# A block of sliding-window attention and a gated MLP on one core: the last bank's causal masks go to VectorE, the input sums start later, and one more gate/up tile leaves the attention stage

## The chip, the cores and the metric

The kernel runs on one core of one Trainium2 chip. The metric is device time in microseconds (us) of the whole program. Three runs of the kernel before took 1064.9, 1059.14 and 1061.83 us, a median of 1061.83 us.

Names used below: PE is TensorE, ACT is ScalarE, DVE is VectorE, POOL is GpSimd, and SP is the engine whose queue issues nearly all transfers. Each engine carries out its own list of instructions strictly in order.

## The reference

For an input x of 2048 tokens by 640 channels the kernel computes a normalised input xn and the sum of three things:

```
xn  = layernorm(x)
q, k, v = split(xn @ wqkv)                  # 32 heads of 20 channels
p   = softmax(q k^T / sqrt(20)), key j visible to query i where 0 <= i - j < 256
out = x + (p v) @ wo
        + (gelu(xn @ w_gate) * (xn @ w_up)) @ w_down      # 1728 hidden channels
```

Everything is float32 to the accuracy of three products per multiplication: each operand is split in a high part and a low part, and high*high, low*high and high*low are summed.

## The kernel before

The program has a start (layer norm, transposes, first projections), an attention stage, a gate/up stage and a last stage of output products.

**Attention stage.** The 32 heads form 8 groups of 4, the tokens 4 chunks of 512 queries. A pair of group and chunk is a *unit*, u = 4 * group + chunk, and there are 32 units (`NU`). The loop `attention()` cuts a unit into 14 *slots* (`NS`). All engines but SP have an order written out by this loop, slot after slot. In a unit stand:

- Score maxima. `max_pair` multiplies queries and keys into two PSUM tiles `ps_m` (L480) and lets DVE reduce each one under the mask tile (L490). There are four `ps_m` buffers. A unit has 8 such pairs: two pairs at slots 5 and 9, and four at slot 0, two of them ahead of the product with v and two behind it.
- Exponentials. `exp_piece` writes scores to `ps_e` (L545) and ACT writes their exponentials to a tile `P` (L547). Twelve pieces, two at each odd slot from 1 to 11, fill three *banks* of four heads each. `pieces(c)` says which key blocks lie in which bank. In the kernel before, the banks are called X, Z, Y in that order, so Y comes last.
- Masks. `clear` runs one slot after a bank is full (slots 4, 8 and 12) and zeroes the entries outside the window with POOL instructions (L558 on the diagonal, L561 at the window's tail), each on 128 rows and 4 x 128 columns. Banks X and Y need three masks each and Z two; in chunk 0 it is two, three and one.
- Product with v. `av_unit` of unit u stands at slot 0 of unit u+1: PE multiplies P by v into `ps_o` (L586), 96 instructions in the trace (64 in chunk 0). `steps_` orders the key blocks.
- Filler. `pull_fill` adds `RATE` / 14 matmuls of other work per slot: the remaining projections of q, k and v and gate/up tiles (`gate_up_fill`), written with L105 into `ps_d` or `ps_v`. The list `sets` orders it. `NFA` says how many of the 14 gate/up tiles have all their columns computed here, in 30 matmuls of 512 columns per chunk, three products for each of 5 row blocks for gate and up.
- Transfers. `load_stack(u+3)` reads the stacked q and k of a later unit back from memory, k at slot 9 (`KSLOT`) and q at slot 12, six transfers each. `x_sums` lets POOL make 8 groups of 10 sums of the input's columns (L724), which the next stage uses; group i starts at slot `XS0 + XSN * i`, one sum every second slot.

**Gate/up stage.** After the last unit the remaining gate/up tiles are computed by `gate_up_pair`, two chunks at a time, with seven half products instead of eight: 54 matmuls of 512 columns for two chunks (L935, `ps_g`) where the filler uses 60. It needs the sums that `x_sums` stored. The last, narrower tile is computed between (`gate_up`, 60 matmuls).

**Last stage.** The outputs are multiplied by w_down and wo (L1202), again with seven products where it can.

The tile scheduler fixes only SP's order here; it places SP's transfers in the order in which it expects them to be ready.

Of the kernel before, what the change touches and what calls it, by code (L numbers as in the profile page):

```python
# [9 lines left out]
F32 = mybir.dt.float32  # L10
# [3 lines left out]
OP = mybir.AluOpType  # L14
# [5 lines left out]
C = 512  # L20
# [7 lines left out]
NEG = -3.0e38  # L28
SR = 3 * DH
QROWS = 64 + SR  # L30
NS = 14
RATE = 35.3
V1_SLOT = 169
MXD = 7
KSLOT = 9
LAG = 3, 5, 4, 4, 4, 4, 3, 3, 4, 3, 2, 1, 1, 1
NFA = 4
HD = D // 2
# [3 lines left out]
WARM = 64  # L42
XS0, XSN = 24, 50
RAMP = 4.0
# [21 lines left out]
def block_kernel(ctx, tc, x, wqk, wv, wgu, wdo, wdl, out):  # L66
    nc = tc.nc
# [57 lines left out]
    mask = st1.tile([128, 320], F32, name="mask")  # L125
    low = qkp.tile([128, C], F32, name="r", tag="r", bufs=1)[:, 0:320]
    for m, off in ((mask, 0), (low, 64)):
        nc.gpsimd.memset(m, 0.0)
        nc.gpsimd.affine_select(out=m, in_=m, pattern=[[1, 320]], compare_op=OP.is_ge,
                                fill=NEG, base=off - 1, channel_multiplier=-1)  # L130
        nc.gpsimd.affine_select(out=m, in_=m, pattern=[[-1, 320]], compare_op=OP.is_ge,
                                fill=NEG, base=256 - off, channel_multiplier=1)
# [379 lines left out]
    def pieces(c):  # L512
        b = 4 * c
        X = [(b, 0, 0, 384)] + ([(b - 2, 384, 0, 128)] if c else [])
        Y = [(b + 1, 0, 128, 384), (b + 3, 384, 384, 128)]
        Z = ([(b - 1, 0, 0, 256)] if c else []) + [(b + 2, 256, 256, 256)]
        return X, Z, Y

# [32 lines left out]
    def clear(u, bi):  # L551
        c = u % NC
        pt = pts[u, bi]
        for p in pieces(c)[bi]:
            for col, diag in diag_tail(*p, c):
                a = pt[:, :, col:col + 128]
# [7 lines left out]
    def av_unit(u):  # L564
# [5 lines left out]
        def half(d, r):  # L570
            i = 2 * d + r
            return d, r, max(0, 64 * i), min(C, 64 * i + 320)

        steps_ = [((0, 0), (0, 1)), ((2, 0), (-1, 1)), ((-1, 0), (2, 1)), ((1, 0), (1, 1)),
                  ((3, 0), (-2, 1)), ((-2, 0), (3, 1))]
        todo = [half(*x) for pair in steps_ for x in pair if x[0] in place]
# [189 lines left out]
    NU = NG * NC  # L766
# [22 lines left out]
    def attention():  # L789
# [16 lines left out]
        for u in range(NU + 1):  # L806
            for i in range(NS):
# [678 lines left out]
```

## Time and profile before

| what | value |
|---|---|
| median of three runs | 1061.83 us |
| the profiled execution | 1063.24 us, span 1061.5 us |
| PE busy | 1040.6 us (98% of the span) |
| DVE busy | 737.3 us (69%) |
| ACT busy | 529.4 us (50%) |
| POOL busy | 372.5 us (35%) |
| mean granted clock of PE | 0.997 |
| first product with v starts | 107.88 us |
| gate/up stage starts (L105 into ps_g) | 583.65 us |
| last stage starts | 817.83 us |

In a group of instructions, the numbers behind the bar are the group's busy time, the mean time of one instruction in ns, and the idle time of the engine just before it with what ended most of that. In a timeline, the columns are start, duration, engine, line and what is written from what; brackets hold idle time before it. In a chain of waits they are start, duration and what ran. PE's matmuls overlap one another, so their mean duration is longer than the step from one to the next.

### The profile page before, as it was taken

The page shows a single profiled execution, that of the slowest core. Times are in us where ns is not written, and L with a number is a line of the kernel's source. Part 1 is how long each engine was busy: PE and PEld are TensorE (multiplying, and loading weights), DVE is VectorE, ACT ScalarE, POOL GpSimd, SP SyncE. Part 2 cuts the span into 40 slices and gives each one's busy share as a digit, 9 for nine tenths or more (in the row PEclk, how much of TensorE's full clock was granted, in tenths as well). Part 3 has the DMA queues.
Part 4 walks back from the last instruction along what each step waited for, and adds up shares of the span by engine and source line. Part 5 has one row for each costly group of instructions (what it writes and reads, how often), then busy time and mean ns, then how long its engine had stood idle before and what let it go on. Part 6 is the DMA issues. An engine that isn't in the chain of part 4 may idle for free.

```text
span 1061.5 us, 25594 instructions
## 1 busy us (share of the span) xinstructions
PE 1040.6 (98%) x9405; PEld 834.0 (79%) x9405; DVE 737.3 (69%) x2007; ACT 529.4 (50%) x1120; POOL 372.5 (35%) x534
## 2 busy tenths in 40 slices
PE   8999999999999999999999999999999999999998
PEld 8878656666678765666666888888888999999998
DVE  7845656665655666687674578877655879988887
ACT  4434667666566665666657532322334543433332
POOL 6021777877564658484846021110110000000000
PEclk9999999999999999999999999999999999999999
DMA  5643355564443335443422647576317874343433
GB/s 197 189 129 94 104 156 146 168 183 128 145 125 100 94 104 170 135 139 97 139 82 67 191 164 250 201 258 230 122 50 259 261 243 134 125 136 101 133 123 111
DMA packets 105191, 158.75 MB, mean 150 GB/s; under 512 B 15420, under 2 KB 60092, under 8 KB 105064
## 3 DMA queue, kind: packets, MB, share of 16 engines
q1 hardware_dynamic: 102680, 150.95, 44.4%
q10 hardware_dynamic: 2384, 6.16, 1.8%
q8 instruction: 74, 1.21, 0.5%
q14 instruction: 53, 0.43, 0.1%
HBM read 101.78 MB, written 54.92 MB: 148 GB/s over the span
## 4 chain that ended last, share of the span: by engine, by line
PE 77%; POOL 6%; DVE 6%; DMA 3%; ACT 3%; SPq 2%; issue 2%; ACTq 0%; DVEq 0%; POOLq 0%
PE ps_g L935 21%; PE ps L1202 17%; PE ps_d L105 17%; PE ps_v L105 6%; PE ps_e L545 6%; PE ps_o L586 4%; PE ps_m L480 4%; POOL pt L247 2%; POOL tx L724 1%; PE ps_g L105 1%; DVE junk L490 1%; POOL P L561 1%; ACT P L547 1%; POOL P L558 1%; POOL wql L627 1%
## 5 line engine op out<-in xcount | busy, mean ns | idle before, releaser
L490 DVE CUSTOM_DVE_ANT_0 junk<-ps_m,mask 128x320 bf16<-128x320 f32 (+2 forms) x512 | 243.1, 475 | 150.8 <-PE ps_m L480 94.4
L547 ACT ACTIVATE P<-ps_e 128x512 f32<-128x512 f32 (+2 forms) x384 | 198.8, 571 | 67.7 <-PE ps_e L545 66.1
L1202 PE MATMUL ps<-wb,at 128*128 128x320 f32 x999 | 156.9, 309 | 1.0 <-DVE at L1040 0.8
L1202 PEld LDWEIGHTS ps<-wb,at 128*128 128x128 f32 x999 | 148.9, 188 | 2.2 <-DVE at L1040 1.3
L545 PE MATMUL ps_e<-qs,ks 124*128 124x128 bf16 (+2 forms) x704 | 117.9, 278 | 1.2 <-ACT P L547 0.9
L558 POOL TENSOR_SCALAR_AFFINE_SELECT P<-P 128x512 f32<-128x512 f32 x128 | 83.4, 652 | 86.8 <-ACT P L547 82.7
L105 PE MATMUL ps_d<-xh,wqh 128*128 128x512 f32 x350 | 109.3, 420 | 0.0
L105 PE MATMUL ps_d<-xh,wql 128*128 128x512 f32 x350 | 108.7, 420 | 0.0
L105 PE MATMUL ps_d<-xl,wqh 128*128 128x512 f32 x350 | 108.4, 418 | 0.0
L1202 PE MATMUL ps<-wt,at 128*128 128x320 f32 x552 | 89.2, 310 | 0.8 <-DVE xr L1225 0.8
L545 PEld LDWEIGHTS <-ks 124*128 124x128 bf16 x704 | 49.7, 98 | 50.4 <-issue 37.3
L586 PE MATMUL ps_o<-P,v 64*32 64x320 f32 (+4 forms) x2816 | 77.6, 349 | 7.7 <-POOL P L561 7.4
L1202 PEld LDWEIGHTS ps<-wt,at 128*128 128x128 f32 x552 | 82.9, 188 | 1.4 <-DVE xr L1225 1.0
L1156 ACT ACTIVATE at<-ss 128x512 fp32r<-128x512 f32 x59 | 37.3, 632 | 86.6 <-DVE ss L1040 86.6
L561 POOL TENSOR_SCALAR_AFFINE_SELECT P<-P 128x512 f32<-128x512 f32 x112 | 72.3, 656 | 21.8 <-ACT P L547 21.8
L98 POOL TENSOR_TENSOR wql<-wr,wqh 128x640 fp32r<-128x640 f32 x11 | 17.6, 1606 | 174.1 <-PE ps_g L935 149.5
L586 PEld LDWEIGHTS ps_o<-P,v 64*32 64x32 f32 x2816 | 46.6, 106 | 36.8 <-POOL P L561 12.4
L105 PEld LDWEIGHTS ps_d<-xh,wql 128*128 128x128 f32 x350 | 64.4, 191 | 12.1 <-issue 1.4
L105 PEld LDWEIGHTS ps_d<-xl,wqh 128*128 128x128 f32 x350 | 63.8, 190 | 11.8 <-issue 1.5
L105 PEld LDWEIGHTS ps_d<-xh,wqh 128*128 128x128 f32 x350 | 63.7, 190 | 11.7 <-issue 1.9
L247 POOL TENSOR_TENSOR pt<-r,pt 128x512 bf16<-128x512 f32 x40 | 46.6, 1165 | 73.5 <-ACT pt L246 65.0
L592 ACT ACTIVATE ob<-ps_o 128x512 f32<-128x512 f32 x32 | 19.1, 598 | 92.7 <-PE ps_o L586 75.8
(195 smaller groups left out, 1923.3 us busy)
## 6 DMA issues: line engine op xcount, KB each, us to landing
hr<-hd SPq DMA_DIRECT2D x104, 128.0 KB
hd<-he SPq DMA_DIRECT2D x50, 256.0 KB
wr<-wgu SPq DMA_DIRECT2D x27, 320.0 KB
qs<-qd SPq DMA_DIRECT2D x64, 120.0 KB
ks<-kd SPq DMA_DIRECT2D x64, 120.0 KB
xi<-x SPq DMA_DIRECT2D x16, 320.0 KB
qs<-qd SPq DMA_DIRECT2D x64, 80.0 KB
ks<-kd SPq DMA_DIRECT2D x64, 80.0 KB
```

The costliest lines, as they stand in the source:

```text
L105: nc.tensor.matmul(ps, a(k), b(k), start=n == 0, stop=n == 3 * nk - 1)
L247: nc.gpsimd.tensor_tensor(out=pt[:, l, :], in0=r, in1=pt[:, 1, :], op=OP.subtract)
L480: nc.tensor.matmul(ps[64 * h:64 * h + 64, col:col + w], q[rows, j, q0:q0 + 64], ks_, start=True, stop=True, tile_position=(64 * r, 64 * h))
L490: nc.vector.tensor_tensor_reduce(out=junk[:, 0:n], in0=ps[:, 320 - n:320], in1=mask[:, 320 - n:320], scale=1.0, scalar=NEG, op0=OP.add, op ...
L545: nc.tensor.matmul(ps[:, col:col + n], k[0:QROWS, j, kc:kc + 128], q[0:QROWS, j, q0:q0 + n], start=True, stop=True)
L547: nc.scalar.activation(pt[:, j, lo:hi], ps[:, lo:hi], AF.Exp, scale=SCALE)
L558: nc.gpsimd.affine_select(out=a, in_=a, pattern=[[0, 4], [1, 128]], compare_op=OP.is_ge, fill=0.0, base=0, channel_multiplier=-1)
L561: nc.gpsimd.affine_select(out=a, in_=a, pattern=[[0, 4], [-1, 128]], compare_op=OP.is_ge, fill=0.0, base=-1, channel_multiplier=1)
L586: nc.tensor.matmul(os[r][32 * j:32 * j + 32, qa:qb], v[rows, w0_:w0_ + 32], pt[rows, j, col + qa - q0:col + qb - q0], start=r not in begun ...
L935: nc.tensor.matmul(ps, i, j, start=first and n == 0, stop=n == len(work) - 1, skip_group_check=True)
L1156: nc.scalar.activation(hi[:, 3:7], s, AF.Copy)
L1202: nc.tensor.matmul(ps[bank][:, 0:HD], *work[bank][j], start=bank not in begun, stop=final[p, bank] == n and j == len(work[bank]) - 1, skip ...
```

## The change

Four things change together.

1. The order of the banks becomes X, Y, Z. Z, with two masks (one in chunk 0), is now the last. `clear` treats it differently: DVE, not POOL, clears it, in two instructions for each mask, one for rows 0 to 63 and one for rows 64 to 127, each 4 x 64 columns wide. Only the 64 columns that lie on the edge for those rows are touched, since the product with v reads no others there. The instruction adds a large number to the mask tile and takes the minimum with P. The mask tile grows by four columns for it. `steps_` reads the key blocks of X and Y first and those of Z last. The four instructions stand on DVE at slot 12.
2. k is loaded at slot 12 together with q (`KSLOT` 12), because bank Z, the last reader of the old k, is now the last bank.
3. The sums of the input start at slot 170 with a step of 33 slots in place of slot 24 and 50.
4. `NFA` goes from 4 to 3: gate/up tile 3 leaves the filler and becomes a tenth tile of `gate_up_pair`. That takes 120 matmuls out of the attention stage and adds 108 to the next one. `RATE` falls from 35.3 to 31.2, so each unit gets 4.1 fillers less.

```diff
-RATE = 35.3
+RATE = 31.2
-KSLOT = 9
+KSLOT = 12
-NFA = 4
+NFA = 3
-XS0, XSN = 24, 50
+XS0, XSN = 170, 33
...
         Z = ([(b - 1, 0, 0, 256)] if c else []) + [(b + 2, 256, 256, 256)]
-        return X, Z, Y
+        return X, Y, Z
...
     def clear(u, bi):
         c = u % NC
         pt = pts[u, bi]
+        if bi == 2:
+            for p in pieces(c)[bi]:
+                for col, diag in diag_tail(*p, c):
+                    for r in (0, 64):
+                        a = pt[r:r + 64, :, col + r:col + r + 64]
+                        m = mask[r:r + 64, 1:65] if diag else mask[r:r + 64, 257:321]
+                        m = m.rearrange("p (o t) -> p o t", o=1).to_broadcast([64, 4, 64])
+                        nc.vector.scalar_tensor_tensor(a, m, -NEG, a, op0=OP.add, op1=OP.min)
+            return
...
-        steps_ = [((0, 0), (0, 1)), ((2, 0), (-1, 1)), ((-1, 0), (2, 1)), ((1, 0), (1, 1)),
-                  ((3, 0), (-2, 1)), ((-2, 0), (3, 1))]
+        steps_ = [((0, 0), (0, 1)), ((1, 0), (1, 1)), ((3, 0), (-2, 1)), ((-2, 0), (3, 1)),
+                  ((2, 0), (-1, 1)), ((-1, 0), (2, 1))]
...
-                if u + 3 < NU and i in (KSLOT, 12):
-                    load_stack(u + 3, (int(i == KSLOT),))
+                if u + 3 < NU and i == KSLOT:
+                    load_stack(u + 3)
```

In the lists below, the lines of the changed kernel behind `clear` carry numbers that are 9 higher than before: L655 is the old L646, L595 the old L586, L609 the old L600. `junk,mx<-ps_m,mask` is one reduction of score maxima, and `mx` behind it reads its result out.

DVE before, from the last group of reductions of unit 25 (slot 9) to the first one of the next unit (slot 0). Two steps of a gate/up tile stand between them:

```order
L490 ISA junk,mx<-ps_m,mask 128x320
L490 ISA mx 128x1
L654 TENSOR_TENSOR gs<-ps_d,gs 128x512
L661 SCALAR_TENSOR_TENSOR he<-he,gs 128x512
L490 ISA junk,mx<-ps_m,mask 128x320
L490 ISA mx 128x1
```

DVE now, at the same place:

```order
L490 ISA junk,mx<-ps_m,mask 128x320
L490 ISA mx 128x1
L655 SCALAR_TENSOR_TENSOR he<-he,gs 128x512
L561 SCALAR_TENSOR_TENSOR P<-mask,P 64x4x64 x4
L490 ISA junk,mx<-ps_m,mask 128x320
L490 ISA mx 128x1
```

The four half masks now stand on DVE ahead of the reductions that belong to slot 0 of the next unit; the steps of the gate/up tile that were there have moved to other slots, since the filler's pace is another.

PE before, at slot 0 behind unit 25: the product with v, and behind it the second two pairs of score maxima:

```order
L480 MATMUL ps_m<-ks_188,qs_182 64x256
L586 MATMUL ps_o<-P,v 32x320 x8
L586 MATMUL ps_o<-P,v 32x256 x8
L586 MATMUL ps_o<-P,v 32x192 x8
L586 MATMUL ps_o<-P,v 32x320 x8
L586 MATMUL ps_o<-P,v 32x128 x8
L586 MATMUL ps_o<-P,v 32x64 x8
L480 LDWEIGHTS qs_182
L480 MATMUL ps_m<-ks_188,qs_182 64x320
```

PE now:

```order
L480 MATMUL ps_m<-ks_188,qs_182 64x256
L595 MATMUL ps_o<-P,v 32x320 x16
L595 MATMUL ps_o<-P,v 32x128 x8
L595 MATMUL ps_o<-P,v 32x64 x8
L595 MATMUL ps_o<-P,v 32x256 x8
L595 MATMUL ps_o<-P,v 32x192 x8
L480 LDWEIGHTS qs_182
L480 MATMUL ps_m<-ks_188,qs_182 64x320
```

The products that read bank Z (256 and 192 columns) have moved from the second place to the last; the score maxima around the product stand where they stood.

SP now, at the load for unit 24 (qd and kd are the stored q and k in memory, qs and ks the tiles that are loaded):

```order
L455 DMA qs_182<-qd_84 60x1024
L256 DMA kd_88<-pt 48x3x512
L256 DMA kd_88<-pt 80x3x512
L455 DMA qs_182<-qd_84 40x1024
L455 DMA qs_182<-qd_84 20x1024
L455 DMA qs_182<-qd_84 60x1024
L455 DMA ks_185<-kd_88 40x1024
L455 DMA ks_185<-kd_88 20x1024
```

SP before, at the same load:

```order
L600 DMA od_92<-ob 20x512 x4
L601 DMA sd_96<-ob 4x512
L455 DMA ks_185<-kd_88 40x1024
L455 DMA ks_185<-kd_88 20x1024
L455 DMA ks_185<-kd_88 60x1024
```

The store of k (`kd_88<-pt`) now stands a few rows ahead of the load that reads it; before, it was stored 46 rows earlier in SP's list.

More of the change, by code (lines that the diff above doesn't have):

```diff
@@ L124, in block_kernel @@
     nc.gpsimd.tensor_copy(identb, ident)
-    mask = st1.tile([128, 320], F32, name="mask")
-    low = qkp.tile([128, C], F32, name="r", tag="r", bufs=1)[:, 0:320]
+    mask = st1.tile([128, 324], F32, name="mask")
+    low = qkp.tile([128, C], F32, name="r", tag="r", bufs=1)[:, 0:324]
     for m, off in ((mask, 0), (low, 64)):
         nc.gpsimd.memset(m, 0.0)
-        nc.gpsimd.affine_select(out=m, in_=m, pattern=[[1, 320]], compare_op=OP.is_ge,
+        nc.gpsimd.affine_select(out=m, in_=m, pattern=[[1, 324]], compare_op=OP.is_ge,
                                 fill=NEG, base=off - 1, channel_multiplier=-1)
-        nc.gpsimd.affine_select(out=m, in_=m, pattern=[[-1, 320]], compare_op=OP.is_ge,
+        nc.gpsimd.affine_select(out=m, in_=m, pattern=[[-1, 324]], compare_op=OP.is_ge,
                                 fill=NEG, base=256 - off, channel_multiplier=1)
```

## The prediction

> **What bounds the kernel now.** I read the page's engine totals first, then the busy times by stage, then the groups of instructions, and last the timeline at the borders between units.
>
> ```profile
> 107.88:554.65 446.77, 438.46 (x5645) 297.36 (x5641) 287.98 (x1059) 285.85 (x621) 296.23 (x441) 1.00 0.44 130
> ...
> 369.14 1.84 PE ps_d L105 x8
> ...
> 597.49 220.34 PE ps_g L935 x972
> ```
>
> The first row is 29 units of the attention stage, 446.77 us or 15.4 us each, with the busy time of PE, of its weight loads, of DVE, ACT and POOL in this order: PE is busy for 438.5 us, 98%, and DVE, ACT and POOL for 64 to 66%. The other two rows are from the chain of waits (start, duration, what ran): the filler runs a matmul every 1.84 / 8 = 0.230 us, the gate/up stage one every 220.34 / 972 = 0.2267 us without a gap. So both stages go at PE's pace, and a matmul that leaves either is worth its 0.23 us, as long as nothing else starts to hold PE.
>
> The timeline at a clean border between two units (25 to 26; rows of other work are left out):
>
> ```profile
> 491.70 1.09 ACT L547 ACTIVATE P<-ps_e 128x512 f32<-128x512 f32 x2 [0.46 <-PE ps_e L545]
> ...
> 492.92 0.64 POOL L558 TENSOR_SCALAR_AFFINE_SELECT P<-P 128x512 f32<-128x512 f32 x1 [2.55 <-ACT P L547]
> ...
> 493.81 0.49 DVE L490 CUSTOM_DVE_ANT_0 junk<-ps_m,mask 128x320 bf16<-128x320 f32 x1 [1.13 <-PE ps_m L480]
> ...
> 493.83 2.45 PE L586 MATMUL ps_o<-P,v 64*32 64x320 f32 x96
> ...
> 495.74 0.49 DVE L490 CUSTOM_DVE_ANT_0 junk<-ps_m,mask 128x320 bf16<-128x320 f32 x1
> 496.16 0.08 DVE L490 DVE_READ_ACCUMULATOR2_ANT mx<- 128x1 f32 x1
> ...
> 496.21 0.47 PE L480 MATMUL ps_m<-ks,qs 60*64 60x320 bf16 x8
> ```
>
> ACT ends the last exponentials at 492.79, the masks start at 492.92, the product with v at 493.83 (all times below are from that start). Beside it DVE reduces four tiles from -0.02 to +2.41. At +2.38 PE comes back to the second pull of score maxima, which needs those four buffers: DVE is just in time, with about 0.1 us to spare, since the pull takes the first two buffers first.
>
> Where the product is shorter, DVE is not in time:
>
> ```profile
> 296.17 1.93 PE L586 MATMUL ps_o<-P,v 64*32 64x320 f32 x64
> ...
> 298.03 0.93 PE L480 MATMUL ps_m<-ks,qs 60*64 60x320 bf16 x8
> ...
> 298.50 0.08 DVE L490 DVE_READ_ACCUMULATOR2_ANT mx<- 128x1 f32 x1
> ```
>
> Behind a chunk 0 the same eight matmuls (L480) take 0.93 us, not 0.47: the last wait for the read-out at 298.50. So PE's second pull waiting for DVE is a mechanism that the trace has already, 0.46 us at each of the 8 borders of this kind unless a mask wait covers it.
>
> **The gate/up tile.** 120 matmuls leave the attention stage: 120 x 0.230 = -27.6 us. 108 join the next: 108 x 0.2267 = +24.5 us. Net -3.1 us. The first number holds only if the units really get shorter, by 4.1 x 0.23 = 0.94 us each.
>
> **The masks that POOL no longer makes.** PE waits for POOL in some products with v. Two rows of the groups, then the timeline at unit 9:
>
> ```profile
> L586 PE MATMUL ps_o<-P,v 64*32 64x320 f32 (+4 forms) x2816 | 77.6, 349 | 7.7 <-POOL P L561 7.4 <-ACT P L547 0.3
> L724 POOL TENSOR_TENSOR tx<-tx,xl 128x256 f32<-128x256 f32 x48 | 35.1, 731 | 0.9
> ...
> 249.34 1.53 PE L586 MATMUL ps_o<-P,v 64*32 64x320 f32 x48
> ...
> 249.83 1.16 POOL L247 TENSOR_TENSOR pt<-r,pt 128x512 bf16<-128x512 f32 x1
> ...
> 252.13 0.63 POOL L558 TENSOR_SCALAR_AFFINE_SELECT P<-P 128x512 f32<-128x512 f32 x1
> 252.22 0.19 PEld L586 LDWEIGHTS ps_o<-P,v 64*32 64x32 f32 x16 [1.73 <-POOL P L561]
> ```
>
> There a 1.16 us split of k (L247) stands ahead of the three masks, and PE stops in the middle of the product for 1.35 us and more. In total the products take 77.6 + 7.7 = 85.3 us; clean they would be 24 x 2.45 + 8 x 1.93 = 74.2 us. So 11.1 us are waits, between unit 1 and the last. Now the last masks on POOL are those of Y, due 6 slots ahead of the product, and the sums of the input (0.73 us each, 80 of them) leave the units 2 to 12, where POOL is fullest. I take back all but 1.0 us of the last unit and 0.5 us for late ones: -9.6 us (bounds 0, if the sums only carry the waits to units 12 to 30, and -11.1).
>
> **The masks on DVE.** What does one cost? The trace has no such instruction; the nearest are sums of the same 256 columns from SBUF. One row of the groups, then timelines at the end of the stage and at two steps of a gate/up tile:
>
> ```profile
> L1040 DVE TENSOR_TENSOR ss<-hr 128x256 f32<-128x256 f32 x59 | 24.9, 422 | 1.3
> ...
> 580.72 0.41 DVE L897 TENSOR_TENSOR sr<-wr 128x256 f32<-128x256 f32 x1
> 581.05 0.85 DVE L897 TENSOR_TENSOR sr<-wr,sr 128x256 f32<-128x256 f32 x1
> ...
> 431.47 0.69 DVE L646 SCALAR_TENSOR_TENSOR he<-he,gs 128x512 f32<-128x512 f32 x1 [0.18 <-ACT he L641]
> ...
> 458.40 0.75 POOL L724 TENSOR_TENSOR tx<-tx,xl 128x256 f32<-128x256 f32 x1
> 458.60 1.09 DVE L646 SCALAR_TENSOR_TENSOR he<-he,gs 128x512 f32<-128x512 f32 x1
> ```
>
> One alone takes 0.42 us; two behind each other start 0.33 us apart. The same L646 takes 0.69 us alone and 1.09 us (1.58 times) when POOL's sums run beside it. So four masks are 3 x 0.33 + 0.42 = 1.41 us, 4 x 0.42 = 1.69 us end to end, or 1.58 x 1.69 = 2.67 us beside POOL. Those 0.33 us are from instructions on all 128 rows, while two masks in a row lie on different halves; I take 1.69 us.
>
> The Trainium skill has a rule on this ("VectorE: DVE Perf Modes", section "Two Vector instructions with no wait between them"): an instruction whose operands start in another group of 32 partitions than those of the one before starts only when all earlier ones have finished. By it the masks, which go from row 0 to row 64 and back, stand end to end (1.69 us), and with 1.41 us instead the sum below would be 15 x 0.3 + 7 x 0.3 = 6.6 us lower. No run here shows it yet.
>
> Behind the masks on DVE's list stand the four reductions that the second pull waits for; ahead of them the masks wait for ACT. They start at 492.92 - 493.83 = -0.91, less 0.13 us since the two slots before hold 0.58 matmuls less: -0.78. They end at +0.91, so the reductions start 0.93 us late, and PE's second pull waits 0.93 - 0.1 = about 0.85 us (0.55 with 1.41 us, 1.8 with 2.67 us). The part of the product that reads Z comes last, after about 1.5 us of 2.45, so the product itself does not wait.
>
> How often? Units of chunk 1 and 3, fifteen with reductions behind them: 15 x 0.85 = 12.8 us. Behind chunk 2 the reductions are narrower (timeline; the last row is a group):
>
> ```profile
> 448.32 2.45 PE L586 MATMUL ps_o<-P,v 64*32 64x320 f32 x96
> ...
> 450.14 0.08 DVE L490 DVE_READ_ACCUMULATOR2_ANT mx<- 128x1 f32 x1
> ...
> L261 DVE TENSOR_TENSOR r<-ps_d,pt 128x512 f32<-128x512 f32 x40 | 27.6, 689 | 34.9 <-ACT pt L265 26.4 <-POOL pt L247 6.6 <-POOL ob L596 1.6
> ```
>
> They are done at 450.22 - 448.32 = 1.90, 0.51 us earlier, so 7 x (0.85 - 0.51) = 2.4 us. Chunk 0 has two masks, done at about +0.06, so its 0.46 us stay, and two that POOL's masks hid come into sight: +0.9 us. At six borders (units 1, 17 to 19, 28, 29) another DVE step of about 0.65 us (L261, or a step of a gate/up tile) now stands between masks and reductions: about +3 us. Sum +19.1 us; bounds +9 us (1.41 us masks, no late steps) and +28 us (half of the borders beside POOL's sums).
>
> **The end of the stage.** In the last unit PE lacked filler:
>
> ```profile
> 577.97 0.87 PE L545 MATMUL ps_e<-qs,ks 124*128 124x128 bf16 x4 [0.59 <-ACT P L547]
> ...
> 579.09 0.87 PE L545 MATMUL ps_e<-qs,ks 124*128 124x128 bf16 x4 [0.26 <-ACT P L547]
> ...
> 580.25 1.90 PE L586 MATMUL ps_o<-P,v 64*32 64x320 f32 x48 [0.29 <-ACT P L547]
> ...
> 582.45 1.20 PE L586 MATMUL ps_o<-P,v 64*32 64x320 f32 x48 [0.31 <-POOL P L561]
> ```
>
> Now 24 fillers are left for this unit where it had 17, and the first three waits (0.59 + 0.26 + 0.29) go: -1.1 us. The last stop inside the product (0.31 us and slower steps) stays.
>
> **The loads at slot 12, the rest.**
>
> ```profile
> 441.03 2.70 SPq L455 DMA_DIRECT2D ks<-kd  x6
> ...
> 444.91 2.63 SPq L455 DMA_DIRECT2D qs<-qd  x6
> ```
>
> From SP's timeline: k and q take 2.7 us of its queue each, at 441.0 and at 444.9 (slot 12). Now k follows q and is issued until about 5.4 us behind slot 12. It is first read at slot 5 of the next unit, seven slots and a product with v later: with (15.4 - 2.45) / 14 = 0.9 us a slot, 8 us behind slot 12. That hides it, except for units 24 to 27, where the store of k stands just ahead (4 x 0 to 2 us). ACT must give its exponentials in shorter slots. Together +0.5 us (0 to +6). With the sums of the input gone from POOL's early units I cost their new place at nothing: POOL has 34% of the stage free to hide it; if that cover goes, Y's masks are late next, priced above.
>
> **Sum.** -3.1 - 9.6 + 19.1 - 1.1 + 0.5 = +5.8 us on the profiled execution's 1063.24 us, so 1069.0 us. That execution lies 1.4 us above the median of 1061.83 us; against the median I forecast 1067.6, rounded 1068 us, 0.6% slower. Below 0.5% (5.3 us) a measurement of this kernel can hardly tell a difference: the three runs themselves differ by 5.8 us.
>
> **Rivals.**
> - *The masks hardly delay DVE* (faster). If they take 1.41 us and start a little earlier, the second pull waits 0.25 us: 15 x 0.25 + 0.9 = 4.7 us in place of 19.1, a sum of -8.6 us, 1053 us. For it: DVE idles 1.13 us before slot 0 in the clean border, so most of a 1.41 us mask fits. Against: that idle time is the wait for ACT's last exponentials, which the masks share. The time falls when all second pulls together cost less than 13.3 us, some 0.6 us at a full border. Chance 0.25.
> - *In between* (same): 1.41 us, no late steps, the second pull costs 11 to 13 us: 1061 us. Chance 0.10.
> - *The masks lock with POOL* (slower). Moved sums and splits run on POOL at slots 12 and 13, and each mask that meets one takes 1.58 times as long, or waits for it to end (L724 0.73 us, L247 1.16 us). At half of the borders the wait is 1.8 us: 28 us in place of 19.1, and with late steps spreading to slots 5 and 9, 1080 us. DVE is busy 288 / 29 = 9.9 us of a 15.4 us unit; with 1.7 us of masks it is 11.6 of 14.5 us, beside the short gaps between its instructions, so it may become the bound in units with a gate/up tile; then the 27.6 us do not come back in full and the tile's move does not do what it says. Chance 0.15. The Trainium skill ("SBUF — State Buffer", section "Who interferes with whom") says that a DVE instruction with two SBUF inputs and a POOL instruction that reads SBUF exclude each other for the whole instruction; the 1.09 us beside 0.69 us agree in kind.
> - *k comes late* at units 24 to 27, with SP held behind a POOL split: 4 x 2 us more, 1076 us. Chance 0.05.
>
> **How the numbers follow.** The forecast has 0.45, of which I put 0.28 above 1067 us and 0.17 within 0.5%. Faster: 0.22 of the first rival's 0.25. Same: 0.17 + 0.10 and the first rival's other 0.03, 0.30. Slower: 0.28 + 0.15 + 0.05 = 0.48. The range reaches to the first rival's time and to the lock's: 1052 to 1080 us; the forecast's own is 1062 to 1074 us.
>
> **What would show it.** In the profile after: ps_g L935 has 1080 matmuls at 0.227 us (not 972), and the stage takes 24.5 us more. The idle time of PE before ps_o that POOL ends falls from 7.7 us to under 2 us. At a full border the second pull (L480, eight matmuls) lasts 1.3 us, not 0.47, and the four masks start 0.42 us apart. I am wrong if the eight matmuls stay near 0.5 us (then faster), if the masks stand 0.6 us apart or the unit is not shorter than 15.0 us (then slower by more), or if PE waits for transfers into ks at slot 5.

## The result: 1101.5 us, 3.8% slower

The changed kernel takes 1101.53 us (median of four runs, 1100.43 to 1103.06) against 1061.35 us of the kernel before. The ratio is 1.038, with a 95% interval of 1.034 to 1.041. I forecast 1068 us with a range to 1080; the time lies 33.5 us above the one and 21.5 us above the other.

**Where the time is.** The starts of the stages, each from its first matmul:

| stretch | before | after | difference | forecast |
|---|---|---|---|---|
| start to first product with v | 107.9 | 104.5 | -3.4 | 0 |
| to the gate/up stage | 475.7 | 493.1 | +17.4 | -18.7 |
| gate/up stage | 234.1 | 258.6 | +24.6 | +24.5 |
| last stage, to the end of the span | 243.8 | 242.2 | -1.6 | 0 |

Most of the -3.4 us in the first row is no effect of the change: the profiled execution before has two stretches of 3.4 us at half clock ahead of the attention stage, at 13.3 and 64.5 us, and the changed one has none there.

The gate/up stage came out as forecast. From the chain of waits of the changed kernel (start, duration, what ran):

```profile
597.63 13.87 PE ps_g L105 x60
611.50 232.57 PE ps_g L944 x1026
```

That is still a matmul every 232.57 / 1026 = 0.2267 us. The whole miss lies in the attention stage. The group of the score maxima in the kernel before:

```profile
L480 PE MATMUL ps_m<-ks,qs 60*64 60x320 bf16 (+3 forms) x1472 | 61.7, 260 | 2.6 <-DVE xl L192 1.1 <-DVE mx L490 0.7
```

and three groups of instructions of the changed kernel:

```profile
L595 PE MATMUL ps_o<-P,v 64*32 64x320 f32 (+4 forms) x2816 | 80.1, 349 | 2.5 <-DVE P L561 1.6 <-POOL P L567 0.6
L480 PE MATMUL ps_m<-ks,qs 60*64 60x320 bf16 (+3 forms) x1472 | 79.4, 261 | 23.3 <-DVE mx L490 21.5 <-DVE xl L192 1.1 <-DMA ks<-kd 0.2
L561 DVE SCALAR_TENSOR_TENSOR P<-mask,P 64x256 f32<-64x256 f32 x112 | 68.3, 610 | 20.8 <-ACT P L547 18.3 <-POOL tx L733 0.6
```

and the row of its waits that answers to them (total, times, longest, in us):

```profile
PE ps_m L480 <- DVE mx L490: 21.5, 64, 1.0
```

PE's idle time ahead of the score maxima (L480) went from 2.6 to 23.3 us, nearly all of it ended by DVE's read-outs (`mx`); PE's idle time ahead of the product with v fell from 7.7 to 2.5 us. The half masks (L561) are new: 112 of them, 68.3 us, 0.610 us each in the mean, where I had taken 0.42.

**A border as I forecast it.** Timeline of the changed kernel between units 25 and 26, the place that the prediction used:

```profile
502.50 1.74 DVE L561 SCALAR_TENSOR_TENSOR P<-mask,P 64x256 f32<-64x256 f32 x4
...
503.45 2.55 PE L595 MATMUL ps_o<-P,v 64*32 64x320 f32 x96
...
505.94 0.46 PE L480 MATMUL ps_m<-ks,qs 60*64 60x320 bf16 x5
...
506.61 0.08 DVE L490 DVE_READ_ACCUMULATOR2_ANT mx<- 128x1 f32 x1
...
506.75 0.33 PE L480 MATMUL ps_m<-ks,qs 60*64 60x320 bf16 x3 [0.35 <-DVE mx L490]
```

Four masks take 1.74 us, 0.43 to 0.45 us from one to the next. PE runs five of the eight matmuls of the second pull, then waits 0.35 us for the read-out at 506.61 and ends the pull at about 507.0: 1.3 us from the product's last matmul to the next work, where the kernel before took 0.54. This is the forecast's border, to 0.1 us.

**Most borders are not like it.** Between units 19 and 20:

```profile
398.49 1.05 POOL L636 TENSOR_TENSOR wql<-wr,wqh 128x128 fp32r<-128x128 f32 x2
...
398.66 2.91 DVE L561 SCALAR_TENSOR_TENSOR P<-mask,P 64x256 f32<-64x256 f32 x4 [1.00 <-ACT P L547]
...
399.07 3.09 PE L595 MATMUL ps_o<-P,v 64*32 64x320 f32 x96
...
399.51 0.91 POOL L733 TENSOR_TENSOR tx<-tx,xl 128x256 f32<-128x256 f32 x1
...
400.50 0.79 POOL L733 TENSOR_TENSOR tx<-xh,tx 128x256 f32<-128x256 f32 x1
...
401.60 1.10 DVE L655 SCALAR_TENSOR_TENSOR he<-he,gs 128x512 f32<-128x512 f32 x1
...
403.17 0.29 PE L480 MATMUL ps_m<-ks,qs 60*64 60x320 bf16 x1 [1.01 <-DVE mx L490]
...
403.81 0.33 PE L480 MATMUL ps_m<-ks,qs 60*64 60x320 bf16 x3 [0.35 <-DVE mx L490]
...
403.82 0.73 POOL L733 TENSOR_TENSOR tx<-xh 128x256 f32<-128x256 f32 x1 [1.66 <-DMA td<-tx]
...
403.90 0.49 DVE L490 CUSTOM_DVE_ANT_0 junk<-ps_m,mask 128x320 bf16<-128x320 f32 x1
...
404.45 0.42 PE L480 MATMUL ps_m<-ks,qs 60*64 60x320 bf16 x1 [0.32 <-DVE mx L490]
...
405.10 0.48 PE L480 MATMUL ps_m<-ks,qs 60*64 60x320 bf16 x3 [0.22 <-DVE mx L490]
```

POOL works on a split of gate/up weights (L636) and on the sums (L733) all through the masks. These take 2.91 us in place of 1.74, a gate/up step behind them (L655) 1.10 us in place of 0.69, and PE gets the pull's matmuls in small portions, each time behind a wait. The pull costs 3.7 us here; the product itself is 0.5 us longer too.

What lengthens a mask is a wait for POOL's instruction to end. The first mask behind unit 11:

```profile
276.42 0.74 POOL L733 TENSOR_TENSOR tx<-xh,xh 128x256 f32<-128x256 f32 x1
276.70 0.74 DVE L561 SCALAR_TENSOR_TENSOR P<-mask,P 64x256 f32<-64x256 f32 x1 [0.53 <-ACT P L547]
```

POOL's sum ends at 277.16, the mask at 277.44. In the changed kernel 53 masks begin while an instruction of POOL with two inputs runs, and 51 of them end 0.27 to 0.29 us behind the end of that instruction, whether 0.12 or 1.11 us of it were left. So a mask's length is set by what is left of POOL's instruction when the mask begins.

**What follows the longest of these.** The granted clock (PEclk, the third value from the right) of the changed kernel in the stretch up to this border, right behind it, and after that:

```profile
399.00:404.10 5.10, 3.74 (x108) 1.98 (x101) 4.72 (x10) 1.36 (x3) 3.28 (x5) 1.00 0.60 192
404.10:410.90 6.80, 6.26 (x21) 3.65 (x18) 3.80 (x15) 2.10 (x5) 2.13 (x3) 0.50 0.19 50
410.90:416.00 5.10, 5.10 (x49) 3.33 (x48) 3.13 (x12) 2.60 (x6) 3.29 (x6) 0.99 0.19 62
```

The clock is halved for 6.8 us. The trace shows four such stretches in the attention stage, at 404.1 (6.8 us), 438.3 (6.8), 458.7 (3.4) and 523.6 (3.4), 20.4 us together; the kernel before has none in this stage. They begin at the borders behind units 19, 21, 22 and 26. There the product and the second pull together take 5.2 to 6.4 us, where a clean border of the kernel before took 2.8. Behind unit 17, with 5.5 us, there is none, so length alone does not decide it. The three later stretches begin 34.1, 54.6 and 119.5 us behind the first, which is 10, 16 and 35 times 3.413 us: in this run the clock changes only at the borders of a fixed grid. The 3.41 us of this grid ahead of each drop, and in the last row one that no drop follows (the second number is PE's busy time):

```profile
400.72:404.13 3.41, 2.05 (x39) 0.91 (x37) 3.08 (x7) 1.39 (x3) 1.67 (x3) 1.00 0.57 178
434.86:438.27 3.41, 2.40 (x68) 1.09 (x53) 3.06 (x7) 1.09 (x2) 2.55 (x4) 1.00 0.67 209
455.34:458.75 3.41, 2.53 (x41) 0.94 (x38) 2.80 (x10) 1.19 (x2) 1.75 (x2) 1.00 0.63 193
520.19:523.60 3.41, 2.28 (x41) 1.05 (x41) 2.57 (x11) 1.09 (x2) 3.18 (x5) 1.00 0.51 162
567.97:571.38 3.41, 2.21 (x77) 1.34 (x54) 2.95 (x9) 1.08 (x2) 2.17 (x4) 1.00 0.09 29
```

PE is busy for 60 to 74% of the time ahead of the drops, and for 65% in the last row, so PE's busy share alone does not decide it either.

**The sum of the stage**, from the starts of the matmuls (for the pull: from the product's last matmul to the first one behind the pull, over 30 borders):

- fillers that left: 120 x 0.230 = -27.6 us;
- second pulls: 20.0 us before, 60.5 us after, +40.5 us. Eight borders behind a chunk 0, with two masks, went from 7.7 to 13.2 us (+5.5). Of the 22 others, five have masks of 1.74 to 1.76 us and stand at 1.40 us in the mean against 0.60 (+4.0); seventeen have masks of 1.89 to 3.90 us and stand at 2.37 against 0.55 (+30.9);
- products with v: 77.7 us before, 71.3 us after, -6.4 us;
- halved clock: half of 20.4 us, +10.2 us at most.

This gives +16.7 us where +17.4 was measured. That it fits so well is partly luck. The stage without its products and pulls is 16.6 us shorter than before. In four runs below whose clock stays whole in the stage (masks back on POOL, the sums replaced, and the two with POOL's reads left out) it is 23.9 to 25.2 us shorter, not 27.6: 116 of the 120 fillers stand behind the first product, 26.7 us, and where the rest went is open. So the halved clock cost 7 to 9 us outside products and pulls; anything more that it cost would lie in products and pulls, which are counted already.

### The profile page after: what moved, and what is told of

Same layout as the page of the kernel before. It is cut to its first block, busy times and chain, and to the rows that moved or that the text cites. A ratio compares the mean times of both kernels' runs of the same rounds, so it can differ in the third digit from the quotient of the medians.

```text
span 1098.4 us, 25705 instructions
## 1 busy us (share of the span) xinstructions
PE 1062.7 (97%) x9393; PEld 844.0 (77%) x9393; DVE 804.6 (73%) x2130; ACT 527.8 (48%) x1120; POOL 343.0 (31%) x470
## 4 chain that ended last, share of the span: by engine, by line
PE 75%; DVE 14%; ACT 4%; issue 3%; DMA 3%; SPq 1%; POOL 0%; DVEq 0%; ACTq 0%; POOLq 0%
PE ps_g L944 21%; PE ps_d L105 17%; PE ps L1211 15%; PE ps_e L545 7%; PE ps_v L105 6%; DVE junk L490 5%; PE ps_m L480 4%; DVE P L561 3%; PE ps_o L595 3%; ACT P L547 2%; PE ps_g L105 1%; DMA stg<-wtd 1%; DVE at L1049 1%; DVE ss L1049 1%; DMA hr<-hd 1%
## 5 line engine op out<-in xcount | busy, mean ns | idle before, releaser
L545 PE MATMUL ps_e<-qs,ks 124*128 124x128 bf16 (+2 forms) x704 | 121.4, 282 | 0.5
L105 PE MATMUL ps_d<-xl,wqh 128*128 128x512 f32 x310 | 102.3, 434 | 0.0
L480 PE MATMUL ps_m<-ks,qs 60*64 60x320 bf16 (+3 forms) x1472 | 79.4, 261 | 23.3 <-DVE mx L490 21.5
L105 PE MATMUL ps_d<-xh,wqh 128*128 128x512 f32 x310 | 100.7, 430 | 0.0
L105 PE MATMUL ps_d<-xh,wql 128*128 128x512 f32 x310 | 99.2, 423 | 0.0
L480 PEld LDWEIGHTS <-qs 60*64 60x64 bf16 x1472 | 34.9, 105 | 79.5 <-issue 77.2
L567 POOL TENSOR_SCALAR_AFFINE_SELECT P<-P 128x512 f32<-128x512 f32 x96 | 62.4, 650 | 81.2 <-ACT P L547 77.8
L561 DVE SCALAR_TENSOR_TENSOR P<-mask,P 64x256 f32<-64x256 f32 x112 | 68.3, 610 | 20.8 <-ACT P L547 18.3
L595 PE MATMUL ps_o<-P,v 64*32 64x320 f32 (+4 forms) x2816 | 80.1, 349 | 2.5 <-DVE P L561 1.6
L247 POOL TENSOR_TENSOR pt<-r,pt 128x512 bf16<-128x512 f32 x40 | 47.3, 1183 | 86.2 <-ACT pt L246 80.7
L595 PEld LDWEIGHTS ps_o<-P,v 64*32 64x32 f32 x2816 | 49.5, 106 | 24.8 <-DVE P L561 4.3
L105 PEld LDWEIGHTS ps_d<-xh,wqh 128*128 128x128 f32 x310 | 58.1, 196 | 9.8 <-issue 0.3
L105 PEld LDWEIGHTS ps_d<-xl,wqh 128*128 128x128 f32 x310 | 58.0, 195 | 9.7 <-issue 0.4
```

What stands on the lines that cost most here:

```text
L105: nc.tensor.matmul(ps, a(k), b(k), start=n == 0, stop=n == 3 * nk - 1)
L247: nc.gpsimd.tensor_tensor(out=pt[:, l, :], in0=r, in1=pt[:, 1, :], op=OP.subtract)
L480: nc.tensor.matmul(ps[64 * h:64 * h + 64, col:col + w], q[rows, j, q0:q0 + 64], ks_, start=True, stop=True, tile_position=(64 * r, 64 * h))
L545: nc.tensor.matmul(ps[:, col:col + n], k[0:QROWS, j, kc:kc + 128], q[0:QROWS, j, q0:q0 + n], start=True, stop=True)
L561: nc.vector.scalar_tensor_tensor(a, m, -NEG, a, op0=OP.add, op1=OP.min)
L567: nc.gpsimd.affine_select(out=a, in_=a, pattern=[[0, 4], [1, 128]], compare_op=OP.is_ge, fill=0.0, base=0, channel_multiplier=-1)
```

## The experiments

Theory A: the masks delay DVE's reductions, PE waits for these at the second pull, POOL's work beside the masks makes them longer, and the halved clock follows the longest waits. The rivals stand in the expectations. All ratios below are to the kernel before, run on the same chip; on the four chips of these runs it took 1060.7 to 1063.2 us.

### One part undone, one part alone

Masks back on POOL at full width, all else as changed:

```diff
     def clear(u, bi):
...
-        if bi == 2:
-            for p in pieces(c)[bi]:
...
-                        nc.vector.scalar_tensor_tensor(a, m, -NEG, a, op0=OP.add, op1=OP.min)
-            return
```

> The changed kernel, with the two masks of the last bank Z given back to POOL at full width; the order X, Y, Z, the later loads of k, the later sums and the moved tile stay. Theory A (the masks on DVE delay the reductions that PE's second pull waits for; after, the waits behind the products with v come to 60.9 us against 20.3 us before, and the clock drops follow them): most of the 40 us goes, 1058 to 1066 us, no stretch at half clock behind 100 us, the second pull at 0.5 us at a full border. Theory B (with 31.2 fillers a unit PE has too little to do and some other engine sets the unit, so the 27.6 us of the moved tile never come back): 1080 to 1095 us, units of 15.0 us or more. Theory C (the later load of k and the later sums cost it): 1080 us or more, with waits of PE for transfers or for POOL.

Measured: 1066.53 us, ratio 1.0032 (1.0017 to 1.0047). Two groups of this run:

```profile
L586 PE MATMUL ps_o<-P,v 64*32 64x320 f32 (+4 forms) x2816 | 78.7, 349 | 11.0 <-POOL P L558 11.0
L480 PE MATMUL ps_m<-ks,qs 60*64 60x320 bf16 (+3 forms) x1472 | 63.2, 260 | 4.1 <-DMA ks<-kd 1.1 <-DVE xl L192 1.1 <-DVE mx L490 0.9
```

35 of the 40 us are gone with the masks on DVE (36.5 us by the ratios), and PE's idle time ahead of the score maxima is back at 4.1 us. Units that took 15.0 to 15.3 us before take 14.2 to 14.5 us here where nothing waits: they do get shorter. So the loss sits in the masks on DVE, as Theory A has it, and the rivals that look for it in the units' length or elsewhere in the change fall. What the rest of the change gains in fillers it loses in waits: the product waits 11.0 us for POOL, 6.6 us of it at units 19, 21, 22, 23 and 26, where the sums now stand, 2.9 us at units 4 to 10 and 1.5 us at the last.

Masks on DVE alone, put into the kernel before (order X, Y, Z and k's load at slot 12 go with them):

```diff
-KSLOT = 9
+KSLOT = 12
...
-        return X, Z, Y
+        return X, Y, Z
```

> The kernel before with only the masks of the last bank on DVE (with the order X, Y, Z and the load of k at slot 12 that belong to it); four gate/up tiles stay in the filler, 35.3 fillers a unit, the sums from slot 24. Theory A: slower than before by 25 to 40 us, 1086 to 1101 us, with mask instructions of 0.42 us alone and 0.8 us beside POOL's two-operand work, more of the latter in the first units where the sums now are. Theory B: the masks cost little while the filler is long, 1058 to 1068 us.

Measured: 1107.58 us, ratio 1.042 (1.0396 to 1.0443), above Theory A's range and no less than the whole change (the two intervals overlap). PE's wait for the reductions in this run:

```profile
PE ps_m L480 <- DVE mx L490: 24.2, 69, 1.5
```

Its masks take 0.607 us in the mean, its second pulls 63.1 us, and its halved stretches in the stage add up to 23.8 us (193 to 603 us). So the loss needs neither the later sums nor the shorter units.

The gate/up tile alone:

```diff
-RATE = 35.3
+RATE = 31.2
-NFA = 4
+NFA = 3
```

> The kernel before with only the gate/up tile moved (three tiles in the filler, 31.2 fillers a unit); masks on POOL in the old order, the sums from slot 24. Theory A: 3.1 us less work on PE, but shorter units leave POOL less time for its last three masks, so 1057 to 1064 us. Theory B: the 24.5 us of the next stage are added and little is taken back, 1075 to 1087 us.

Measured: 1068.95 us, ratio 1.0056 (1.0041 to 1.0071), above Theory A's range and below Theory B's. The products with v took 84.5 us in place of 77.7; the row of their waits:

```profile
PE ps_o L586 <- POOL P L561: 13.4, 11, 2.4
```

It was 7.4 us before. Shorter units leave POOL less time for its masks ahead of the product; that is the likely reason, and no run isolates it. The longer products take back more than the tile's 3 us. Here too the clock is halved twice in the stage, 3.4 us each, at 199.2 and 451.8 us: inside a product of 5.3 us and at the end of one of 4.9 us, in place of 2.2. Another of 4.9 us, at 178.7, has no drop.

### What makes the masks long

In the changed kernel, the 80 sums of the input are replaced by a memset (the sums are left out of the result):

```diff
-            nc.gpsimd.tensor_tensor(out=o, in0=i, in1=j, op=op)
+            nc.gpsimd.memset(o, 1.0)
```

> The changed kernel, with the 80 sums of the input on POOL replaced by writes of a constant into the same tiles at the same slots: the sums are left out, so that POOL reads nothing from SBUF there. Theory A with contention (49 of 112 masks took 0.82 us in place of 0.42 us, since POOL instructions that read two SBUF operands ran beside them): masks beside a write of a constant stay at 0.42 us, fewer than 30 of 112 stay long (beside splits of k and of weights), mean 0.50 us or less, and the time falls by 8 to 20 us to 1082 to 1093 us. Rival (DVE is simply full, whatever POOL does): mask mean near 0.61 us and time within 4 us of 1101 us.

Measured: 1082.37 us, ratio 1.0188 (1.0171 to 1.0205), 19 us less than the changed kernel, and no halved stretch in the stage. The masks, a little above the 0.50 us that was expected at most:

```profile
L561 DVE SCALAR_TENSOR_TENSOR P<-mask,P 64x256 f32<-64x256 f32 x112 | 58.2, 520 | 20.9 <-ACT P L547 19.0
```

Of the 112, 23 are still longer than 0.46 us (49 in the changed kernel), 20 of them at units 1 to 10 and 21 to 23, where POOL's splits of q and k (L247) and of gate/up weights (L636) stand at slots 12 and 13. The next run replaces these by a memset too:

```diff
-            nc.gpsimd.tensor_tensor(out=pt[:, l, :], in0=r, in1=pt[:, 1, :], op=OP.subtract)
+            nc.gpsimd.memset(pt[:, l, :], 0.0)
...
-            nc.gpsimd.tensor_tensor(out=lo[:, k], in0=raw[:, k], in1=hi[:, k].bitcast(F32), op=OP.subtract)
+            nc.gpsimd.memset(lo[:, k].bitcast(F32), 0.0)
```

> The changed kernel with three kinds of POOL work replaced by a memset of the same tile: the 80 sums of the input, the 40 splits of q and k, and the splits of the gate/up weights in the filler (the low parts and the sums are left out of the result). Theory A: the masks were long because POOL's instructions with two inputs stood beside them. Where only the sums were left out, 23 of 112 masks stayed long and 12 full borders stood at 2.0 to 2.5 us; now all full borders come to the clean 1.3 us: 12 x 0.9 = 11 us less than the 1082 us of that run and some 2 us of the product, 1069 us (1062 to 1074), with a mean mask of 0.43 us and no halved clock. Rival G: what lengthens the masks is ACT, PE's reading of P or a transfer: the mean mask stays at 0.5 us or more, 1078 to 1084 us.

Measured: 1069.89 us, ratio 1.0087 (1.0065 to 1.0109). Masks and pull:

```profile
L561 DVE SCALAR_TENSOR_TENSOR P<-mask,P 64x256 f32<-64x256 f32 x112 | 47.2, 421 | 21.9 <-ACT P L547 18.4 <-POOL wql L636 1.4
L480 PE MATMUL ps_m<-ks,qs 60*64 60x320 bf16 (+3 forms) x1472 | 72.2, 261 | 12.2 <-DVE mx L490 9.6 <-DVE xl L192 1.2
```

One mask of 112 is long, beside a two-input instruction of POOL that is left in, the mean is 0.421 us, and no clock is halved in the stage. So it is POOL's instructions that read their inputs, and nothing of ACT, PE or the transfers, that lengthen the masks. Eight masks of this run have a memset of POOL beside them and take 0.417 us. In the changed kernel the 63 masks with a two-input POOL instruction beside them take 0.76 us in the mean, 1.38 at most; the 49 others take 0.42. POOL's instruction need not have two inputs: in the run with the other order of half masks below, a mask that begins beside an `affine_select` (L570, one input, ends at 447.72) ends at 447.99, 0.27 us behind it too. The Trainium skill ("SBUF — State Buffer", section "Who interferes with whom") says just that: a DVE instruction with two inputs from SBUF contends with a POOL instruction that reads SBUF, not with one that only writes it. The trace agrees. The same three replacements with bank Z's masks on POOL are the measure for what the clean masks cost (the edit is the sum of those shown for the masks, the sums and the splits):

> The same three replacements in the changed kernel with bank Z's masks on POOL. It is the measure for the other run: POOL, much emptier, no longer makes the product wait (11 us of waits before), so 1066.5 - 11 = 1055 us (1050 to 1060). Theory A: the other run is 12 to 18 us slower than this one, which is what clean masks of 0.43 us on DVE cost by themselves (22 borders x 0.7 us = 15 us). Rival G: 25 us or more between them.

Measured: 1053.50 us, ratio 0.9933 (0.9918 to 0.9948). The masks on DVE thus cost 1069.9 - 1053.5 = 16.4 us where nothing lengthens them, and 1101.5 - 1066.5 = 35.0 us beside POOL's work. POOL's work beside the masks is worth the other 18.6 us, the halved clock that comes with it included; the 35.0 us are between runs on different chips, so this is good to 2 us or so.

### The order of the half masks

Both masks of rows 0 to 63 first, then both of rows 64 to 127:

```diff
-            for p in pieces(c)[bi]:
-                for col, diag in diag_tail(*p, c):
-                    for r in (0, 64):
+            for r in (0, 64):
+                for p in pieces(c)[bi]:
+                    for col, diag in diag_tail(*p, c):
```

> The changed kernel with the four half masks in another order: both of rows 0 to 63 first, then both of rows 64 to 127. If a mask is held until the one before has ended only when it lies on the other half, two of three steps fall from 0.43 to about 0.33 us: 0.2 us a border less in 24 borders, 1096 us (1093 to 1100). If all steps stay at 0.43 us, the time stays at 1101 us. The masks that meet POOL's instructions stay long either way (some 49 of 112).

Four masks that meet no POOL work, behind the same unit, in the changed kernel:

```profile
306.43 1.74 DVE L561 SCALAR_TENSOR_TENSOR P<-mask,P 64x256 f32<-64x256 f32 x4 [0.55 <-ACT P L547]
```

and in this order:

```profile
304.44 1.54 DVE L561 SCALAR_TENSOR_TENSOR P<-mask,P 64x256 f32<-64x256 f32 x4 [0.55 <-ACT P L547]
```

The steps are 0.342, 0.439 and 0.342 us in place of 0.431, 0.436 and 0.449 (medians of 6 to 10 undisturbed ones each). Only the step that changes the half stays. The rule that the prediction cited from the Trainium skill ("VectorE: DVE Perf Modes", section "Two Vector instructions with no wait between them") holds here. The time is 1096.72 us, ratio 1.0337 (1.0289 to 1.0385); the point lies where it was expected, but the interval overlaps that of the changed kernel, so the gain of 5 us is not shown by the times.

### Another place for the second pull

If PE waits because the reductions are late, a later pull should free it. The second two pairs go from behind the product at slot 0 to slot 2:

```diff
-                if i in (0, 5, 9) or T == 3:
+                if i in (0, 5, 9) or T == 3 or i == 2 and u:
                     pull_max(2, T)
                 if i == 0 and u:
                     av_unit(u - 1)
-                    pull_max(2, T)
```

In the changed kernel:

> The changed kernel with the second two pairs of score maxima moved from behind the product with v at slot 0 to slot 2, so that DVE has two slots more for masks and reductions. Theory A (the masks delay the reductions, PE waits for them at the second pull, the halved clock follows those waits): from the last product-with-v matmul to the next matmul behind the pull PE took 60.5 us over 30 borders where 8 matmuls at 0.06 us are 30 x 0.5 = 15 us; some 40 us of waits go, and the 10 us of halved clock with them: 1050 us (1045 to 1062), less than the kernel before. Theory D (DVE itself is the bound of the units, wherever the pull stands): the waits come back at slot 2 or 5: 1085 to 1100 us.

In the kernel before:

> The kernel before with the same move of the pull and nothing else. Theory A: only its own small waits can go, 20.0 - 15 = 5 us at most: 1058 to 1063 us, so the move by itself is worth little and what e7 gains beyond it belongs to the masks on DVE. If the move is worth 20 us or more here too, e7 says nothing on the masks.

In the changed kernel with bank Z's masks on POOL:

> The changed kernel with bank Z's masks back on POOL at full width, and the pull at slot 2. Theory A: the pull's waits (23.8 - 15 = 9 us at most) go, the product's waits for POOL's masks (12 us) stay: 1058 to 1064 us, slower than e7 by about the product's waits. Theory D gives the same; if this is faster than e7, masks on DVE are a loss even where nothing waits directly behind them.

| second pull | masks of Z on POOL | masks of Z on DVE |
|---|---|---|
| slot 0, behind the product | 1066.53 (1.0032) | 1101.53 (1.0376) |
| slot 2 | 1090.19 (1.0255) | 1088.88 (1.0252) |

All three times miss Theory A's forecasts, and 1088.88 us lies in the range of Theory D. What speaks against D is that PE's waits for DVE's read-outs came to 5.3 us in that run, in place of 21.5. With the pull at slot 2 the masks on DVE cost nothing on balance (-1.3 us, inside the intervals), with the pull behind the product they cost 35 us: the loss goes through that pull. But the move is no gain: it makes the kernel before 20 us slower too (1081.79 us, ratio 1.0184, 1.0169 to 1.0199), which I had put at nothing. Timeline of that run at slot 9:

```profile
439.19 0.23 PE L507 MATMUL ps_n<-identb,nm 128*128 128x128 bf16 x1
439.35 0.46 PE L480 MATMUL ps_m<-ks,qs 60*64 60x320 bf16 x5
...
440.17 0.25 ACT L509 ACTIVATE mr<-ps_n 32x128 bf16<-32x128 f32 x1
...
440.47 0.33 PE L480 MATMUL ps_m<-ks,qs 60*64 60x320 bf16 x3 [0.66 <-ACT mr L509]
```

The transpose of the maxima (L507) uses one of the four PSUM buffers of the score maxima, until ACT has copied it (L509). It is due seven slots behind a unit's last pair, so the move took it from slot 7 to slot 9, right ahead of the pull there. The next runs put it back to slot 7, in the changed kernel and in the kernel before:

```diff
-                at(slot + (MXD if slot >= 0 else 4), max_end, x[0])
+                at(slot + (MXD - (2 if slot % NS == 2 else 0) if slot >= 0 else 4), max_end, x[0])
```

> The changed kernel with the second pull at slot 2, as one run before, but with the transpose of the maxima kept at slot 7. In the run before the move of the pull had carried that transpose from slot 7 to slot 9, just ahead of the pull there, where PE then waited for DVE's reductions and for ACT's copy of the transposed maxima. Theory A with this side effect (E): the 18 us that the move cost the kernel before go here too: 1089 - 18 = 1071 us (1060 to 1075). Rival F: the move costs what it costs because DVE's reductions of slot 2 and slot 5 now stand too close, and the transpose is innocent: 1085 to 1092 us.

> The kernel before with the same two moves (pull at slot 2, transpose of the maxima at slot 7). E: 1081.8 - 18 = 1064 us (1058 to 1066), so that the pull's place is worth little by itself. F: 1079 to 1084 us.

Measured: 1079.69 us, ratio 1.0154 (1.0122 to 1.0187), and 1071.58 us, ratio 1.0095 (1.0061 to 1.013). Both lie between the two theories: the transpose is worth 9 to 10 us of the 20, the rest of the move's cost stays. What it is was not tested; in the trace of the second run PE changes from a filler to a pull 30 times more (117 for 87), and all its steps that begin with a filler take 11.5 us more than before. In the changed kernel with both moves most of the waits have gone:

```profile
L561 DVE SCALAR_TENSOR_TENSOR P<-mask,P 64x256 f32<-64x256 f32 x112 | 68.4, 611 | 18.8 <-ACT P L547 16.3 <-POOL tx L733 0.6
L480 PE MATMUL ps_m<-ks,qs 60*64 60x320 bf16 (+4 forms) x1472 | 68.1, 262 | 5.3 <-DVE mx L490 3.1 <-DVE xl L192 1.1 <-DMA ks<-kd 0.5
```

The masks are as long as in the changed kernel (0.611 us), yet PE waits only 3.1 us for the reductions, and no clock is halved in the stage.

The same in the changed kernel with the sums of the input at their old slots:

```diff
-XS0, XSN = 170, 33
+XS0, XSN = 24, 50
```

> The changed kernel with the pull at slot 2, the transpose at slot 7, and the sums of the input back in the units 0 to 30 of before (slot 24, step 50, in place of 170 and 33). If the sums cost by lengthening the masks that stand beside them, the cost stays when they are spread out, and the time is that of the run with the transpose at slot 7 within 4 us. If the product with v waits again for POOL in units 2 to 12, up to 8 us more.

Measured: 1079.64 us, ratio 1.0159 (1.0135 to 1.0183). The place of the sums moves nothing here.

The changed kernel with pulls at slots 0, 3, 6 and 10, the transpose at slot 8:

```diff
-                at(slot + (MXD if slot >= 0 else 4), max_end, x[0])
+                at(slot + (MXD - (2 if slot % NS == 3 and slot > 3 else 0) if slot >= 0 else 4), max_end, x[0])
...
-                if i in (0, 5, 9) or T == 3:
+                if i in (0, 3, 6, 10):
                     pull_max(2, T)
                 if i == 0 and u:
                     av_unit(u - 1)
-                    pull_max(2, T)
```

> The changed kernel with the pulls spread evenly, at slots 0, 3, 6 and 10 in place of 0, 0 (behind the product), 5 and 9, and the transpose of the maxima at slot 8. Theory A: PE's waits for reductions go almost entirely, the halved clock too: 1062 us (1050 to 1072). Rival D (DVE's own list is full in units with a gate/up tile): PE waits for it wherever the pulls stand, 1080 us or more.

Measured: 1083.57 us, ratio 1.0199 (1.0177 to 1.0221). Theory A's forecast is missed, and the time lies in Rival D's range. But PE waits only 3.2 us for the reductions, not as Rival D would have it; the product now waits for the masks:

```profile
PE ps_o L595 <- DVE P L561: 4.0, 6, 1.8
PE ps_m L480 <- DVE mx L490: 3.2, 9, 0.5
```

Those 4.0 us explain a part of what it lies above the run before; the rest is open. No version that computes the whole reference beats the kernel before.

## Why the prediction was wrong

- **The gate/up tile** (-3.1 us). The +24.5 us in the gate/up stage are there (+24.6). The -27.6 us are rather -24 to -25 us in the attention stage, by the four runs with a whole clock there, and four of the 120 matmuls stand ahead of it, about -0.9 us. So this part is worth 1 us or less rather than 3.
- **The waits for POOL's masks** (-9.6 us). -6.4 us. POOL's waits went, as forecast (one of 0.6 us is left), but "the product itself does not wait" was wrong: in nine units the masks on DVE ended 2.1 to 3.1 us behind the product's start and made it 0.1 to 1.1 us longer, 5.1 us together.
- **One mask, one clean border.** Right. 0.42 us each, end to end; 1.74 us for four (1.69 forecast); 1.3 us for the pull at a full border, which the prediction named. With no long masks the masks cost 16.4 us in all, where this term said 19.1. The 1.58 times that the prediction read beside POOL's sums is no factor, though: the instruction waits for POOL's to end, so its length depends on when it begins.
- **How many borders are clean: the step that failed.** The term took clean masks at every border ("I take 1.69 us"), and only its upper bound set half of the borders beside POOL's sums, +28 us. The price beside POOL was about right: 2.6 to 3.0 us for twelve of the seventeen long borders (2.67 forecast), and the seventeen wait 1.82 us more than before in the mean (1.8 forecast). Their number was not: 17 of 22. The bound looked at POOL's sums alone; the rival named the splits too, but also stopped at half. A split (L247 or L636) stands beside the masks at fourteen of the seventeen, the sums alone at three; the row of 1.16 us ahead of the masks at unit 9, which the prediction quotes, showed one of them. The term is +40.5 us in place of +19.1.
- **The halved clock.** +7 to +10 us, in no term and in no rival.
- **The end of the stage, k's loads.** PE waited 0.2 us for a load of k, so the low chance of "k comes late" stands, and nothing is seen of the +0.5 us beyond it. In the last unit PE's three waits for ACT are gone, as the -1.1 us had it; one wait for POOL of 0.6 us is left there.

Of the rivals, "the masks lock with POOL" (0.15) had the mechanism and the right side; its 1080 us were too low, since it too stopped at half of the borders, and its last part, units that do not get shorter, did not happen. "The masks hardly delay DVE" fell: even clean masks cost 16 us.

## What to carry to other kernels

An instruction that is moved to another engine is priced at the place where it will stand: list, unit by unit, what an engine that can block it (here POOL) runs in those microseconds, since an average share of the stage says nothing about them. Where work goes ahead of something that is just in time (here 0.1 us to spare), every lengthening is paid almost in full by whoever waits. And before a consumer is moved out of the way, look at what is timed relative to it: the transpose came along with the pull and made a new wait.

## What the hardware showed that I had not expected

- The granted clock fell to half for 3.4 or 6.8 us in the middle of a stage in which PE is 98% busy before, without any single wait above 1.01 us. It came at borders where a slow product and several short waits took 5 us and more together. The Trainium skill ("TensorE: Matmul & The Clock Gate", section "Part 1: The HAM clock gate") gives a window of about 3.4 us over which activity is watched, and counts a whole idle window as what drops the clock. The lengths, one and two such windows, agree; but here the 3.41 us ahead of the first drop, with waits of 1.01 and 0.35 us between matmuls and PE busy for 60%, were enough, so no idle window is needed. What share of a window it takes, and whether the kind of matmul counts, is open, and that the waits cause the drop is shown only by its absence where they are gone.
- Four runs of the kernel with grouped rows took 1091.99, 1096.88, 1096.56 and 1105.05 us with mean clocks of 0.998, 0.994, 0.991 and 0.988: the same kernel's time spreads by 13 us, and the clock falls with it from run to run. How often it fell in each is known only for the first, whose trace has one stretch of 3.4 us in the stage.
- DVE's two-input step L655 and the masks are lengthened alike beside POOL (1.10 for 0.69 us, 0.6 to 1.4 for 0.42 us), while its reductions from PSUM keep their 0.49 us at the same border, also beside POOL's sums (the row at 403.90 beside the one at 403.82).
